# Attention block on one core: half of each head's third probability tile goes through TensorE, and two engines copy it out

## The chip, the cores and the metric

The kernel runs on one core of a Trainium2 chip. The metric is device time in microseconds, from the start of the program to its end, as the median of several runs. Beside the timed runs there is one profiled execution, whose trace all views below come from.

A core has five engines that run their own instruction streams and meet through semaphores: TensorE (PE; its weight loads are shown as PEld), VectorE (DVE), ScalarE (ACT), GpSimd (POOL) and SyncE (SP), which here only issues DMAs. TensorE writes to PSUM; the other data lies in SBUF.

## The reference

A block with adaptive layer norm: attention with 32 heads over a given key and value cache, then a mixer and an MLP. What matters here is the attention; x has 2048 rows of 640, q, k and v have 32 heads of 2048 rows of 128.

```python
def _A_ref(x, k_cache, v_cache, wq, wo):
    q = (x @ wq).reshape(B, Sq, H, Dh).transpose(0, 2, 1, 3)
    scores = jnp.einsum('bhqd,bhkd->bhqk', q, k_cache) * Dh ** (-0.5)
    p = _softmax(scores, axis=-1)
    o = jnp.einsum('bhqk,bhkd->bhqd', p, v_cache)
    return o.transpose(0, 2, 1, 3).reshape(B, Sq, H * Dh) @ wo
...
mod = (_silu(c) @ w_mod).reshape(c.shape[0], 6, 1, -1)
...
h = _layernorm(x, axis=-1) * (1 + ca) + sa
x = x + ga * _A_ref(h, A_k_cache, A_v_cache, A_wq, A_wo)
h = _layernorm(x, axis=-1) * (1 + cb) + sb
x = x + gb * _B_ref(h, B_w1, B_w2, B_w3, B_w4)
```

## The kernel before

**Steps and tiles.** The attention is one loop of steps `s` (L544). A head has 16 query tiles of 128 rows, so there are 512 tiles; step `s` makes the scores of tile `s` (128 rows by 2048 keys) and works on earlier tiles too. Tile `g` has the number `g % 16` within its head; "step 5 of a head" is the step that makes the scores of its tile 5.

**What a step issues**, engine by engine:

- TensorE: in each of two half steps two score matmuls of 512 keys (`qk`, L287, recorded as L294 and L15) into one half of the score buffer in PSUM, then eight matmuls of the product with V for tile `s - 8` (`pv`, L300, recorded as L307), then, in some half steps, one further piece. The piece is either one of five matmuls that make 512 columns of the next head's Q (`q_piece`, L242), or four 128x128 transposes (`t_piece`, L255, recorded as L261).
- VectorE: two passes (L588), one for each half of the scores. Each scales 1024 columns, writes them to `negS` in SBUF and keeps the row minimum. `negS` has three buffers.
- GpSimd: the smaller of the two minima (L598), and later the normalising of finished tiles (L448, L455) and their store to a scratch tensor (L462).
- ScalarE: every second step a copy of two finished output tiles out of PSUM (L579), copies out of the two small PSUM banks, then the exponential over 2048 columns (L601), which writes the probabilities `Pb` as bf16.
- SP: DMAs, in the order in which the loop adds them.

**Transposed probabilities.** `pv` needs the probabilities with keys on partitions (`PTs`). For 14 of a head's 16 tiles this is a DMA transpose from SBUF to SBUF (`transpose`, L228, recorded as L230): tiles 0 and 1, 4 and 5, 6 and 7, 8 and 9, 12 and 13, 14 and 15 in pairs, tiles 2 and 11 alone. Tiles 3 and 10 (`PE_TILES`) are transposed by TensorE in two halves of 1024 columns, three and four steps after their scores. Each half fills one of two small PSUM banks (`Oaug`, `QPp`), which the Q pieces use too, in turn (`bank`, L236). The bank is copied to `PTs` by `t_evac` (L265): by ScalarE (L270) in three of the four cases, ahead of that step's exponential; by VectorE (L272) for the second half of tile 3, after that step's two score passes (`by_dve`, L274). This VectorE copy stands at the end of step 7 of each head, once per head, and so serves as a mark in the trace.

**Q pieces.** `taken` (L276) lists the half steps, counted from 0 to 31 in a head, that hold transposes; groups of five Q pieces are put around them. A finished group is cast to bf16 by ScalarE (`q_evac`, L249, recorded as L252).

**SP's order in a head.** Pair (0, 1) and tile 2, then the K load of the next head (L213, at step 2), pair (4, 5), the load of the Q weights (L217), pairs (6, 7) and (8, 9), the V load (L222), tile 11, pairs (12, 13) and (14, 15).

**Order between engines.** `Prog._add` (L34) works out the waits from names: every operation lists the names it reads (`r`) and writes (`w`). An operation waits for the last writer of what it reads, and for the last writer and the readers of what it writes, if these are on another engine. The name of a half of a transposed tile is `("PT", slot, half)`, with ten slots (`RP`); that of a small bank is `("J", bank)`.

## Time and profile before

| what | value |
|---|---|
| median of three runs | 1581.96 us (1580.96 to 1587.68) |
| profiled execution, its own time | 1586.91 us |
| its span | 1585.1 us |
| granted TensorE clock | 0.998 |
| score passes L588, VectorE | 1024, mean 1220 ns |
| exponentials L601, ScalarE | 512, mean 2017 ns |
| P·V matmuls L307, TensorE | 8192, mean 220 ns |
| ScalarE's bank copies L270 | 96 of 1024 bf16 columns, mean 1.02 us |
| VectorE's bank copies L272 | 32 of 1024 bf16 columns, mean 686 ns |
| ScalarE's casts L252 | 128 of 512 columns, mean 0.58 us |
| transposing DMAs L230 | 256, median 7.0 us from issue to landing |

How to read it: the attention loop runs from about 40 to about 1268 us; the rest is the mixer and the MLP. A mean is the time from start to end of one instruction. Instructions of one engine overlap a little, so that the distance from one start to the next is shorter than the mean where the engine runs without a gap; that distance is read from the timeline. A transposing DMA shows two times: its entry on SP's queue, and the time from issue to landing.

### The profile page before, as it was taken

Reading aid. Unit: us, or ns where it says so; the run is one execution under the profiler, and the core shown is the slowest. Engines: PE = TensorE matmul, PEld = TensorE weight load, DVE = VectorE, ACT = ScalarE, POOL = GpSimd, SP = SyncE. Lnnn points to the kernel's source line nnn. Section 1 sums busy time; section 2 is a strip of 40 time slices with the busy share of each in tenths; the row PEclk is TensorE's granted clock in tenths of the full one; section 3 lists DMA queues with packets and bytes.
Section 4 is the critical chain, followed back from the end, with each engine's and each line's share of the span. In section 5 each row is a group of like instructions: output and inputs, shape, how many; then the busy total and the mean of one; then the engine's idle time right before and its main releaser. Section 6 shows DMA issues by size and latency. Waiting matters only on the chain.

```text
span 1585.1 us, 33308 instructions
## 1 busy us (share of the span) xinstructions
PE 1466.2 (92%) x13822; PEld 910.2 (57%) x13047; DVE 1395.5 (88%) x2463; ACT 1275.2 (80%) x1113; POOL 624.6 (39%) x1396
## 2 busy tenths in 40 slices
PE   4899998998999999899999999999999899999999
PEld 2466655655655556566566566656656655554545
DVE  6999999999999999999999999999999927667535
ACT  4999999999999999999999999999999900034230
POOL 0144444444444444444444444444444423323100
PEclk9999999999999999999999999999999999999999
DMA  9999999999999999999999999999999998735100
GB/s 294 239 235 237 239 234 231 252 231 223 240 233 236 233 242 239 235 246 233 235 244 236 239 245 237 236 244 240 242 238 243 236 245 184 157 55 141 39 25 34
DMA packets 1189435, 338.76 MB, mean 214 GB/s; under 512 B 1169888, under 2 KB 1183264, under 8 KB 1189280
## 3 DMA queue, kind: packets, MB, share of 16 engines
q1 hardware_dynamic: 1180800, 315.49, 100.0%
q0 software_dynamic: 6144, 16.79, 3.6%
q10 hardware_dynamic: 2336, 4.34, 0.8%
q8 instruction: 107, 1.75, 0.5%
q14 instruction: 48, 0.39, 0.1%
HBM read 43.48 MB, written 19.40 MB: 40 GB/s over the span
## 4 chain that ended last, share of the span: by engine, by line
DVE 26%; ACT 25%; PE 20%; DMA 17%; issue 9%; POOL 2%; SPq 0%; ACTq 0%; POOLq 0%; DVEq 0%
DVE negS L588 24%; ACT ring L601 20%; DMA ring<-ring 16%; PE Sps L532 7%; PE Sps L835 4%; ACT ring L270 2%; PE Oaug L786 2%; PE QPp L786 2%; PE Sps L771 1%; ACT kv L252 1%; PE PTp L307 1%; ACT Of L579 1%; DMA hTx<-o_scratch 1%; POOL small L598 1%; DVE ring L372 1%
## 5 line engine op out<-in xcount | busy, mean ns | idle before, releaser
L588 DVE TENSOR_SCALAR_CACHE_REDUCE negS<-Sps 128x1024 f32<-128x1024 f32 x1024 | 1178.5, 1220 | 35.2 <-PE Sps L15 34.2
L601 ACT ACTIVATE ring<-negS,small 128x2048 bf16<-128x2048 f32 x512 | 1029.7, 2017 | 25.1 <-POOL small L598 23.2
L307 PEld LDWEIGHTS PTp<-kv,ring 128*128 128x128 bf16 x8192 | 551.7, 98 | 370.2 <-DMA ring<-ring 95.2
L307 PE MATMUL PTp<-kv,ring 128*128 128x129 bf16 x8192 | 645.5, 220 | 49.5 <-DMA ring<-ring 48.9
L15 PE MATMUL Sps<-kv 128*128 128x512 bf16 x1024 | 387.9, 379 | 14.2 <-DVE negS L588 8.6
L598 POOL TENSOR_SCALAR small<-small 128x1 f32<-128x1 f32 x512 | 147.1, 287 | 633.3 <-DVE negS L588 633.2
L294 PE MATMUL Sps<-kv 128*128 128x512 bf16 x926 | 356.1, 385 | 24.3 <-DVE negS L588 12.8
L455 POOL TENSOR_SCALAR On<-Of,small 128x128 bf16<-128x128 f32 x512 | 191.6, 375 | 13.0
L294 PEld LDWEIGHTS Sps<-kv 128*128 128x128 bf16 x1024 | 98.2, 96 | 123.2 <-DVE negS L588 102.0
L448 POOL TENSOR_TENSOR small<-Of,small 128x4 f32<-128x4 f32 x128 | 133.4, 1042 | 9.8 <-ACT Of L579 9.7
L462 POOL DMA_DIRECT2D o_scratch<-On x128 | 103.1, 806 | 40.8 <-POOL On L455 37.2
L579 ACT COPY Of<-PTp 128x259 f32<-128x259 f32 x256 | 95.9, 374 | 14.1 <-PE PTp L307 14.1
L245 PE MATMUL Oaug<-hTx,kv 128*128 128x512 bf16 x264 | 100.1, 384 | 4.8 <-DVE hTx L404 4.8
L245 PE MATMUL QPp<-hTx,kv 128*128 128x512 bf16 x259 | 96.7, 378 | 3.2 <-ACT hTx L399 2.5
L716 ACT ACT_TABLE_LOAD x1 | 1.3, 1283 | 114.0 <-POOL hTx L734 114.0
L588 DVE DVE_READ_ACCUMULATOR negS<-Sps 128x1 f32 x1024 | 85.1, 83 | 0.0
L635 POOL TENSOR_SCALAR negS<-negS 128x1 f32<-128x1 f32 x48 | 24.5, 510 | 129.9 <-DVE negS L644 129.9
L532 PE MATMUL Sps<-wo,hTx 128*128 128x512 bf16 (+1 forms) x502 | 69.3, 297 | 2.7 <-DMA hTx<-o_scratch 2.2
L532 PE MATMUL Sps<-wo,negS 128*128 128x128 bf16 (+1 forms) x503 | 69.9, 298 | 0.5
L270 ACT COPY ring<-Oaug 128x1024 bf16<-128x1024 bf16 x64 | 65.3, 1020 | 0.0
L839 DVE TENSOR_TENSOR ring<-Sps,ring 128x640 f32<-128x640 f32 x15 | 12.4, 824 | 57.4 <-PE Sps L835 57.4
L649 DVE TENSOR_TENSOR ring<-Sps,mod_bc 128x640 f32<-128x640 f32 x16 | 13.1, 821 | 55.3 <-PE Sps L532 33.4
(88 smaller groups left out, 1018.3 us busy)
## 6 DMA issues: line engine op xcount, KB each, us to landing
kv<-in_A_v_cache_dram SPq DMA_DIRECT2D x32, 512.0 KB, 5.0
o_scratch<-On POOLq DMA_DIRECT2D x128, 128.0 KB, 3.9
kv<-in_A_wq_dram SPq DMA_DIRECT2D x32, 160.0 KB, 3.1
wo<-in_A_wo_dram SPq DMA_DIRECT2D x1, 5120.0 KB, 17.6
ring<-ring SPq DMA_TRANSPOSE x256, 7.0
ring<-in_A_x_dram SPq DMA_DIRECT2D x5, 640.0 KB, 7.1
ring<-in_w_mod_dram SPq DMA_DIRECT2D x1, 3200.0 KB, 14.1
out_dram<-wo SPq DMA_DIRECT2D x15, 160.0 KB, 1.8
```

Source lines behind the costliest of these rows:

```text
L15: return t.add_instruction(mybir.InstMatmult(name=t.bass.get_next_instruction_name(), ins=[t.lower_ap(rhs), t.lower_ap(lhsT)], outs=[t.low ...
L245: G.op("tensor", lambda t: t.matmul(JB[jb], wq[:, hb, q, :], hT[:, q, cc * 512:(cc + 1) * 512], start=(q == 0), stop=(q == KT - 1)), r=[(" ...
L294: ins = (t.matmul if c2 == 0 else partial(same_weights, t))(Sps[:, col:col + 512], QT[:, hb, j * 128:(j + 1) * 128], KTs[:, hb, col:col + ...
L307: ins = t.matmul(ob[:, 0:129], PTs[:, b, kt, :], Vaug[:, hb, kt, 0:129], start=(kt == 0), stop=(kt == NKT - 1))
L448: G.op("gpsimd", lambda g: g.tensor_tensor(out=rl[:, 4 * b:4 * b + 4], in0=Of[:].rearrange("p a z d -> p (a z) d")[:, 4 * b:4 * b + 4, 128 ...
L455: G.op("gpsimd", lambda g: g.tensor_scalar(out=On[:, b, z, :], in0=Of[:, 2 * b + z // 2, z % 2, 0:128], scalar1=rl[:, 4 * b + z:4 * b + z ...
L462: G.dma("gpsimd", lambda e: e.dma_start(o_scr[jj // 2:jj // 2 + 2, :, hh].rearrange("a p z d -> p a (z d)"), On[:, b].rearrange("p (a z) d ...
L532: ins = t.matmul(YB[b][:, c0:c0 + cw], OTj[pr % 2][:, 2 * hh + z, :], wo[:, hh, c0:c0 + cw], start=(hh == 0), stop=(hh == H - 1))
L579: G.op("scalar", lambda a, p=p: a.copy(Of[:, p % 4].rearrange("p z d -> p (z d)")[:, 0:259], PO[:, (p % 2) * 512:(p % 2) * 512 + 259]), r= ...
L588: G.op("vector", lambda v, half=half, s=s, r8=r8: v.tensor_scalar(out=negS[:, s % 3, half * 1024:(half + 1) * 1024], in0=Sps[:, half * 102 ...
L598: G.op("gpsimd", lambda g, r8=r8: g.tensor_scalar(out=nm[:, r8:r8 + 1], in0=nm0[:, r8:r8 + 1], scalar1=nm1[:, r8:r8 + 1], scalar2=None, op ...
L601: G.op("scalar", lambda a, s=s, r8=r8: a.activation(Pb[:, s % RP, :], negS[:, s % 3, :], ACT.Exp, bias=nm[:, r8:r8 + 1], scale=-1.0), r=[( ...
```

## The change

Each head's tile 2 (`PE_HALF = 2`) is split. Its first 1024 columns are still transposed by a DMA, in the same place of SP's order, of half the size (`transpose_half`). Its second 1024 columns are transposed by TensorE as two pieces of four 128x128 transposes in step 5 of the head, one in each half step, into one small bank. The bank is copied out in two parts (`h_evac`): ScalarE copies the first 512 columns ahead of its exponential of step 5, VectorE the other 512 after its two score passes of step 5. Both copies list `("PT", slot, 1)` as written. Half steps 10 and 11 are added to `taken`. The small banks now serve nine groups a head where they served eight.

```diff
+                PE_HALF = 2
...
+                def transpose_half(g):
+                    b = g % RP
+                    G.dma("sync", lambda e: e.dma_start_transpose(PTs[:, b, 0:8, :], ring[:, b, 0:1024]),
+                          ("t", b), r=[("Pb", b)], w=[("PT", b, 0)])
...
-                taken = [u for j in PE_TILES for u in range(2 * (j + 3), 2 * (j + 5))]
+                def h_evac(g, part):
+                    jb = bank(("t", g, 1))
+                    dst = PTs[:, g % RP, 8 + 4 * part:12 + 4 * part, :]
+                    src = JBb[jb][:, 512 * part:512 * part + 512].rearrange("p (k q) -> p k q", k=4)
+                    if part == 0:
+                        G.op("scalar", lambda a: a.copy(dst, src), r=[("J", jb)], w=[("PT", g % RP, 1)])
+                    else:
+                        G.op("vector", lambda v: v.tensor_copy(dst, src), r=[("J", jb)], w=[("PT", g % RP, 1)])
+                half_of = lambda g: 0 <= g < NG and g % NQT == PE_HALF
+
+                taken = [u for j in PE_TILES for u in range(2 * (j + 3), 2 * (j + 5))] + [2 * (PE_HALF + 3), 2 * (PE_HALF + 3) + 1]
...
+                        if half_of(s - 3):
+                            t_piece(s - 3, 1, half)
...
                     for fn, x, y in evacs:
                         if fn is q_evac or not by_dve(x, y):
                             fn(x, y)
+                    if half_of(s - 3):
+                        h_evac(s - 3, 0)
...
                     for fn, x, y in evacs:
                         if fn is t_evac and by_dve(x, y):
                             fn(x, y)
+                    if half_of(s - 3):
+                        h_evac(s - 3, 1)
...
-                        if not is_pe(s):
+                        if half_of(s):
+                            transpose_half(s)
+                        elif not is_pe(s):
```

## The prediction, made before the changed kernel ran

> **What bounds the kernel now.** I read the busy table first, then the groups, the waits, the queues, and the timeline of single heads. The page's first parts leave four candidates: TensorE, VectorE and ScalarE are each busy most of the span, and queue q1, which carries the transposes, is full.

> ```profile
> PE 1466.2 (92%) x13822; PEld 910.2 (57%) x13047; DVE 1395.5 (88%) x2463; ACT 1275.2 (80%) x1113; POOL 624.6 (39%) x1396
> ...
> q1 hardware_dynamic: 1180800, 315.49, 100.0%
> ```

> In the timeline one VectorE score pass (L588, half a tile) follows the last at 1.145 us, its busy 1.22 us overlapping. A head has 32 of them, and one bank copy (L272) that holds VectorE for 0.605 us: 32 x 1.145 + 0.605 = 37.24 us. That copy marks step 7 of each head. Its 32 occurrences are 37.2 to 40.0 us apart, 1186.8 us over 31 intervals, mean 38.28. So many heads run exactly at VectorE's floor and others are about 2 us longer. The 33 us above 31 floors are these waits:

> ```profile
> DVE negS L588 <- PE Sps L15: 34.2, 44, 2.3
> ...
> PE PTp L307 <- DMA ring<-ring: 48.9, 59, 2.0
> ```

> The P·V matmuls (L307) wait for a transposed tile, the next scores come late, and VectorE stands. The transposes are late because SP's queue runs behind the work:

> ```profile
> 864.41 2.02 SPq L213 DMA_TRANSPOSE kv<-in_A_k_cache_dram  x1
> 866.48 5.00 SPq L230 DMA_TRANSPOSE ring<-ring  x1
> 871.51 0.58 SPq L217 DMA_DIRECT2D kv<-in_A_wq_dram  x1
> 872.14 4.41 SPq L230 DMA_TRANSPOSE ring<-ring  x1
> ```

> The K load belongs to step 2, but the step-7 copy of that head was at 864.86: SP is five steps late, its entries end to end. The pair issued at 872.14 lands 7.6 us later, when the chain of waits has P·V start. One K load follows the last by 38.4 us on average. So the head's pace is set by the DMA queue, with VectorE 1 us below it, and ScalarE close: its exponentials follow each other at 1.905 us, the output copies L579 take 0.26, the Q casts L252 0.47, the bank copies L270 0.895: 16 x 1.905 + 8 x 0.26 + 4 x 0.47 + 3 x 0.895 = 37.1 us.

> **The change, part by part.** *DMA.* One single-tile transpose per head becomes half of one; number and order of SP's entries stay. A pair takes 4.1 to 4.5 us of the queue, half a tile a quarter of that, 1.0 to 1.1 us; at worst nothing, if time went by entries. The queue then needs 37.3 us a head (38.3 at worst).

> *TensorE.* Eight transposes more per head, in step 5. Four of them are shown in one row at 0.39 us, and the next matmul can start after about 0.23:

> ```profile
> 128.04 0.63 PE L307 MATMUL PTp<-kv,ring 128*128 128x129 bf16 x8
> 128.51 0.39 PE L261 MATMUL Oaug<-ident,ring 128*128 128x128 bf16 x4
> ```

> Scores 0.44, P·V 0.47, transposes 0.23: 1.14 us per half step, just inside VectorE's 1.145. Half steps 10 and 11 carry no other piece now, and blocking them moves no Q piece (the third group of five starts at 16 either way). I take nothing, covered by VectorE; uncovered it is 2 x 0.23 us a head, 15 us. [...]

> *ScalarE.* A copy of 512 bf16 columns: no row has it. Half of L270's 0.895 is 0.45, the cast of 512 f32 columns is 0.47: I take 0.47 (at most 0.895). ScalarE's work becomes 37.6 us.

> *VectorE.* A copy of 512 columns: between half of L272's 0.605 and all of it; I take 0.34. The floor becomes 37.57 us.

> *The added wait.* Both copies name ("PT", slot, 1) as written. The scheduler makes a later writer wait for an earlier one on another engine, so VectorE's copy, queued after its step 5, waits until ScalarE's is complete. ScalarE's stands behind exponential 4 and the output copy. This is where they are in a head without a DMA wait (VectorE first):

> ```profile
> 127.46 1.22 DVE L588 TENSOR_SCALAR_CACHE_REDUCE negS<-Sps 128x1024 f32<-128x1024 f32 x1
> 128.61 0.08 DVE L588 DVE_READ_ACCUMULATOR negS<-Sps 128x1 f32 x1
> ```
> ```profile
> 127.56 2.05 ACT L601 ACTIVATE ring<-negS,small 128x2048 bf16<-128x2048 f32 x1
> 129.46 0.41 ACT L579 COPY Of<-PTp 128x259 f32<-128x259 f32 x1
> 129.72 2.06 ACT L601 ACTIVATE ring<-negS,small 128x2048 bf16<-128x2048 f32 x1
> 131.62 1.06 ACT L270 COPY ring<-Oaug 128x1024 bf16<-128x1024 bf16 x1
> ```

> VectorE is through step 5 at 128.61. ScalarE's new copy would go where exponential 5 starts, 129.72, and be complete some 0.56 later (the casts' length); with 0.05 of signal VectorE copies at 130.33, 1.72 us late. In the heads that had a DMA wait ScalarE had caught up, and the same reckoning gives 1.0 to 1.1. Behind the waiting copy stand all of VectorE's score passes: step 6, then exponential 6, TensorE's scores of step 7.

> Does it repeat at full price? I follow one head from the moment VectorE's copy starts (0). VectorE ends step 6 at 0.34 + 2.29 = 2.63, step 7 at 4.92, step 8 (after L272) at 7.81, then every 2.29 up to step 5 of the next head at 37.57. An exponential starts at least 0.51 after its step ends (866.61 + 1.145 to 868.26 in another head). ScalarE runs exponential 5 and the copy of tile 3 until 2.66, waits 0.5 for step 6, 0.1 for 7, about 1.0 for 8, 0.1 for 9, then is never idle again: the casts, the two copies of tile 10 and the output copies put it behind. 37.6 of work and 1.75 idle bring its new copy's end to 39.3. The two engines, each with about 37.6 us of work, now meet once a head and cannot lend each other their slack: period about 39.35 us, 1.8 us of it VectorE's wait.

> *The sum*, against the profiled execution (span 1585.1, its own time 1586.9): 31 x (39.35 - 38.28) = +33.2; first head's step 5, 0.81 + 0.34 = +1.2; the DMA wait of the last eight steps goes, -1.1. The queue at 37.3 (or 38.3) is faster than 39.35, so its lag is gone by the end: the last pair is issued at 1273.0 while its exponential ended about 1268.1, -5 us in the tail (0 at least). Together +28: 1615 from this execution, 1610 from the median of the runs, 1582.0, which is 5 us lower. The new pace holds no DMA waits, the likely source of that spread, so I go between: **1612 us**. By bounds: copies at half length take 2 to 3 us off (1607), no tail gain adds 5.

> **Rivals.** *Relief wins.* If VectorE's copy waited for nothing, the new floor would be 37.57, above the relieved queue: 31 x (37.57 - 38.28) = -22, tail and rest -6: about 1556. For it: the queue is the bound now. Against: even with ScalarE starved, exponential 4 starts 0.51 after step 4, and 0.51 + 1.905 + 0.26 + 0.56 + 0.05 is 1.0 us after step 5; the two halves share one writer key. [...]

> *Short wait.* If ScalarE keeps catching up, the wait is 1.05: period 38.6, 31 x 0.35 = +11, less 5: 1588 to 1593. For it: 19 of the 32 heads show about that lag now. Against: they show it because DMA waits held VectorE back, and these go.

> *Long copies.* If small copies cost nearly as much as whole ones, 0.27 and 0.43 more per head both lie on the meeting path: +22, about 1634. A queue that is still late at times would add less. For it: nothing measured at 512 bf16 columns; against: the casts at 0.47.

> **Chances.** Forecast 0.66 (1600 to 1621), relief 0.10, short wait 0.14, long copies 0.10. A range of 1588 to 1625 holds the forecast, most of the short wait and part of the long copies: 0.8. A difference under 0.5%, 8 us, can't be told from none here. Faster by more: 0.11 (relief). Within: 0.07 (half of the short wait). Slower: 0.82.

> **What would show it.** VectorE's new copy x32 with about 1.7 us idle before each, released by ScalarE (some 50 us); ScalarE's idle before L601 up from 25 to about 70 us, released by GpSimd (L598); P·V's DMA waits and VectorE's waits for scores nearly gone; step-7 copies evenly 39.3 apart; SP waiting for ScalarE in earnest. I am wrong if that idle is under 0.3 us each, or if the DMA waits stay as they are.

## The result and the profile after

The changed kernel takes 1630.77 us (1628.73 to 1632.19, five runs) against 1583.02 us: ratio 1.029, 95% interval 1.0268 to 1.0311. It is slower, as forecast, but by 48 us where I had 30, and the time lies above the range. The profiled execution has a span of 1630.0 us, 44.9 us more than before.

The busy table and the queues:

```profile
PE 1524.3 (94%) x14327; PEld 959.7 (59%) x13303; DVE 1408.8 (86%) x2495; ACT 1292.3 (79%) x1145; POOL 622.3 (38%) x1396
...
q1 hardware_dynamic: 1148032, 307.10, 93.4%
```

The transposing queue is no longer full, yet the kernel is slower: something else bounds it. The groups (busy us, mean ns of one, idle time before them and what ended it):

```profile
L607 DVE TENSOR_SCALAR_CACHE_REDUCE negS<-Sps 128x1024 f32<-128x1024 f32 x1024 | 1178.5, 1221 | 14.7 <-PE Sps L15 14.1
L622 ACT ACTIVATE ring<-negS,small 128x2048 bf16<-128x2048 f32 x512 | 1030.6, 2021 | 56.0 <-POOL small L619 54.6
...
L322 PE MATMUL PTp<-kv,ring 128*128 128x129 bf16 x8192 | 660.0, 224 | 1.1 <-ACT Of L596 1.1
```

P·V (now L322) waits for no DMA any more, where it waited 48.9 us. VectorE waits 14 us for scores instead of 34. ScalarE stands idle for 56 us before its exponentials, nearly all of it for the minima that GpSimd makes; before, it was 25:

```profile
L601 ACT ACTIVATE ring<-negS,small 128x2048 bf16<-128x2048 f32 x512 | 1029.7, 2017 | 25.1 <-POOL small L598 23.2
```

The table of waits has a new line, VectorE's copy waiting for ScalarE's, 32 times, 1.66 us each:

```profile
DVE ring L288 <- ACT ring L286: 53.2, 32, 1.8
```

In the timeline of one head, first VectorE, then ScalarE:

```profile
528.87 0.08 DVE L607 DVE_READ_ACCUMULATOR negS<-Sps 128x1 f32 x1
530.66 0.42 DVE L288 COPY ring<-Oaug 128x512 bf16<-128x512 bf16 x1 [1.71 <-ACT ring L286]
531.00 1.21 DVE L607 TENSOR_SCALAR_CACHE_REDUCE negS<-Sps 128x1024 f32<-128x1024 f32 x1
```
```profile
527.82 2.06 ACT L622 ACTIVATE ring<-negS,small 128x2048 bf16<-128x2048 f32 x1
529.72 0.42 ACT L596 COPY Of<-PTp 128x259 f32<-128x259 f32 x1
529.98 0.65 ACT L286 COPY ring<-Oaug 128x512 bf16<-128x512 bf16 x1
530.45 2.07 ACT L622 ACTIVATE ring<-negS,small 128x2048 bf16<-128x2048 f32 x1
```

VectorE is through step 5 at 528.87. ScalarE's copy starts behind exponential 4 and the output copy, ends at 530.63, and VectorE copies at 530.66. The copies cost 0.34 us (530.66 to 531.00) and 0.47 us (529.98 to 530.45).

The step-7 copies of VectorE are 39.78 us apart on average, against 38.28 before. But they aren't even: 39.35 in the first two heads, later about 39.46, 39.86 and 40.13 in turn. In the two that take longer VectorE waits for scores again, once in step 7 (0.57 us at 256.06) or twice in step 8 (0.16 us each, at 297.64 and 299.04). TensorE's timeline shows why (the head of the two views above; the second and third line have the same shape of matmul):

```profile
529.92 0.38 PE L266 MATMUL QPp<-ident,ring 128*128 128x128 bf16 x4
532.28 0.39 PE L309 MATMUL Sps<-kv 128*128 128x512 bf16 x1 [1.98 <-DVE negS L607]
...
535.40 0.63 PE L309 MATMUL Sps<-kv 128*128 128x512 bf16 x1
```

While VectorE stands, TensorE has nothing to do for 1.98 us. Three microseconds later the same matmul takes 0.63 instead of 0.39 us. Windows of 1 us, first from a head in which this does not happen, then from the head before it, in which it does (the last three columns are the granted clock, the DMA share and the GB/s):

```profile
core 0: us, PE busy (x) PEld busy (x) DVE busy (x) ACT busy (x) POOL busy (x), PEclk, DMA share, GB/s
...
453.00:454.00 1.00, 1.00 (x15) 0.83 (x13) 1.00 (x3) 0.96 (x2) 0.01 (x1) 1.00 0.23 49
454.00:455.00 1.00, 1.00 (x15) 0.74 (x13) 1.00 (x3) 0.70 (x1) 0.61 (x2) 1.00 0.82 190
...
413.00:414.00 1.00, 1.00 (x15) 0.80 (x13) 1.00 (x3) 0.98 (x2) 0.00 (x0) 1.00 1.21 262
414.00:415.00 1.00, 1.00 (x8) 0.53 (x5) 1.00 (x3) 0.67 (x1) 0.62 (x2) 0.57 0.96 218
415.00:416.00 1.00, 1.00 (x13) 1.00 (x10) 1.00 (x3) 1.00 (x1) 0.00 (x0) 0.50 1.25 286
416.00:417.00 1.00, 1.00 (x6) 0.34 (x4) 0.91 (x3) 0.97 (x3) 0.62 (x2) 0.50 1.22 280
417.00:418.00 1.00, 1.00 (x11) 0.74 (x8) 0.92 (x1) 1.00 (x1) 0.78 (x1) 0.72 1.19 273
```

The granted clock is halved from 414.1 to 417.6. The 44.9 us of span are thus: 31 x (39.34 - 38.28) = 33 for the meeting of the two engines, 31 x 0.44 = 13 to 14 on top, which I put down to the clock, and -1.4 for the ends.

### The profile page after: what moved, and what is told of

It reads as the page before. It is cut to its first block, busy times and chain, and to the rows that moved or that the text cites. A ratio compares the mean times of both kernels' runs of the same rounds, so it can differ in the third digit from the quotient of the medians.

```text
span 1630.0 us, 34069 instructions
## 1 busy us (share of the span) xinstructions
PE 1524.3 (94%) x14327; PEld 959.7 (59%) x13303; DVE 1408.8 (86%) x2495; ACT 1292.3 (79%) x1145; POOL 622.3 (38%) x1396
## 4 chain that ended last, share of the span: by engine, by line
ACT 56%; PE 24%; DVE 14%; issue 4%; POOL 1%; DMA 0%; ACTq 0%; POOLq 0%
ACT ring L622 45%; DVE negS L607 11%; PE Sps L547 9%; ACT kv L257 4%; ACT ring L275 4%; PE Sps L858 3%; ACT Of L596 3%; PE PTp L322 2%; PE QPp L809 2%; PE Oaug L809 2%; PE Sps L794 1%; PE Sps L309 1%; PE Sps L15 1%; ACT ring L286 1%; DVE ring L288 1%
## 5 line engine op out<-in xcount | busy, mean ns | idle before, releaser
L322 PEld LDWEIGHTS PTp<-kv,ring 128*128 128x128 bf16 x8192 | 572.8, 100 | 294.9 <-issue 83.7
L322 PE MATMUL PTp<-kv,ring 128*128 128x129 bf16 x8192 | 660.0, 224 | 1.1 <-ACT Of L596 1.1
L309 PE MATMUL Sps<-kv 128*128 128x512 bf16 x1024 | 401.2, 392 | 80.4 <-DVE negS L607 77.1
L15 PE MATMUL Sps<-kv 128*128 128x512 bf16 x1024 | 395.4, 386 | 0.0
L250 PE MATMUL Oaug<-hTx,kv 128*128 128x512 bf16 x320 | 121.7, 385 | 1.9 <-ACT hTx L414 1.3
L250 PE MATMUL QPp<-hTx,kv 128*128 128x512 bf16 x320 | 120.7, 381 | 2.7 <-ACT hTx L414 2.3
L477 POOL DMA_DIRECT2D o_scratch<-On x128 | 103.1, 806 | 40.8 <-POOL On L470 37.2
L547 PE MATMUL Sps<-wo,hTx 128*128 128x128 bf16 (+1 forms) x512 | 70.7, 299 | 0.0
L266 PE MATMUL QPp<-ident,ring 128*128 128x128 bf16 x640 | 65.2, 227 | 0.0
L266 PE MATMUL Oaug<-ident,ring 128*128 128x128 bf16 x640 | 64.7, 226 | 0.0
```

Source lines behind the costliest of these rows:

```text
L15: return t.add_instruction(mybir.InstMatmult(name=t.bass.get_next_instruction_name(), ins=[t.lower_ap(rhs), t.lower_ap(lhsT)], outs=[t.low ...
L250: G.op("tensor", lambda t: t.matmul(JB[jb], wq[:, hb, q, :], hT[:, q, cc * 512:(cc + 1) * 512], start=(q == 0), stop=(q == KT - 1)), r=[(" ...
L266: ins = t.transpose(JBb[jb][:, z * 128:(z + 1) * 128], Pb[:, g % RP, kt * 128:(kt + 1) * 128], ident[:])
L309: ins = (t.matmul if c2 == 0 else partial(same_weights, t))(Sps[:, col:col + 512], QT[:, hb, j * 128:(j + 1) * 128], KTs[:, hb, col:col + ...
L322: ins = t.matmul(ob[:, 0:129], PTs[:, b, kt, :], Vaug[:, hb, kt, 0:129], start=(kt == 0), stop=(kt == NKT - 1))
L547: ins = t.matmul(YB[b][:, c0:c0 + cw], OTj[pr % 2][:, 2 * hh + z, :], wo[:, hh, c0:c0 + cw], start=(hh == 0), stop=(hh == H - 1))
```

## The experiments

Theory W: VectorE's wait for ScalarE's copy sets a head's length, and the gap that it leaves in TensorE's work halves TensorE's clock for a while. Theory T: TensorE, with eight transposes more and no slack in a half step, is the bound, and its clock is low because it has more work. Each run stands beside runs of the kernel before on the same chip; ratios are to those. The runs are from several chips, so two versions are compared by their ratios; a ratio of 0.01 is about 16 us.

**1. VectorE's copy one step later.** By then ScalarE's copy is long done.

```diff
-                    if half_of(s - 3):
-                        h_evac(s - 3, 1)
+                    if half_of(s - 4):
+                        h_evac(s - 4, 1)
```

> VectorE's copy of the 512 columns moves behind its passes of step 6, everything else as in the changed kernel. Theory W (the wait of VectorE for ScalarE's copy costs the time, and TensorE, idle for 2 us behind it, then runs at a lower granted clock): no wait before the copy, granted clock back at 0.99 or more, period of a head 37.6 us, 1555 to 1572 us, faster than before. Theory T (eight more transposes overload TensorE, whose half step had no slack, and lower its clock): period still above 39, clock near 0.97, 1620 us or more. If the copies themselves cost more than 0.34 and 0.47 us: between, 1575 to 1600.

Measured: 1575.02 us, ratio 0.9958 (0.9941 to 0.9974), clock 0.998. Of the 31 heads 13 take 37.55 us, where the forecast's floor for VectorE was 37.57; the mean is 37.91. What is left above the floor are DMA waits, as the lines of its table of waits show:

```profile
PE PTp L322 <- DMA ring<-ring: 18.8, 38, 1.1
...
DVE negS L607 <- PE Sps L15: 14.7, 21, 2.2
```

All transposes, copies and the relief of the queue are the changed kernel's; only the place of one copy differs, and the ratio falls from 1.029 to 0.996, by some 53 us. T falls. The time is 3 us above the range that W had, and at the edge of the one for dearer copies; but the heads at 37.55 us show that the copies cost what was forecast. What W had left out are the DMA waits, which did not vanish (see run 5).

**2. and 3. TensorE kept busy in its gap.** The second half of the scores of step 6 is made again, with the same values, while TensorE would stand idle: four times more in run 2, whose edit is shown, and once more in run 3.

```diff
                         if half_of(s - 3):
                             t_piece(s - 3, 1, half)
+                        if half_of(s - 4) and half == 1:
+                            for _ in range(4):
+                                qk(s, 1)
```

> The changed kernel; TensorE makes the second half of the scores of step 6 four times more (1.7 us, same values), in the gap in which it stands idle. Theory W: VectorE's wait of 1.7 us stays, TensorE's gap shrinks from 2.0 to about 0.3 us, the clock stays at 0.99 or more, all heads take 39.35 us: 1614 to 1620 us, 13 us under the changed kernel. Theory T: more work for TensorE, the same or a lower clock, 1631 us or more. If the extra 0.43 us a head comes from neither: 1629 to 1633.

Measured: 1620.36 us, ratio 1.0239 (1.022 to 1.0258), clock 0.997. More work for TensorE, and by the ratios some 8 us less than the changed kernel. W's range ended at 1620.

> The run that kept TensorE busy, with one repetition of the scores instead of four: TensorE's gap is then about 1.55 us, between 1.97 (the changed kernel, clock halves in two heads of three) and 1.30 (the wait alone, all heads alike). If the gap's length decides and 1.55 is short enough: 39.34 us in every head, 1618 to 1622 us. If any such gap lets the clock fall: 1629 to 1633.

Measured: 1616.14 us, ratio 1.023 (1.0211 to 1.025), 2 us below the range expected for a gap that is short enough. The views of the cores and of the waits:

```profile
core 0: 1613.8 us, clock 0.998
```
```profile
DVE ring L288 <- ACT ring L286: 53.1, 32, 1.8
```

VectorE's wait is the same to 0.1 us in all, but nearly every head takes 39.34 us in both runs, and the clock holds (1.00 from 60 to 1280 us in run 3, 0.97 from 60 to 1290 us in the changed kernel). So the 0.44 us a head are the clock's, and the gap of 1.97 us is what lowers it; with one pair of matmuls in it, 0.43 us, the gap is about 1.54 us (an estimate, 1.97 - 0.43), and the clock stays up. The 4 us between the two runs lie outside the 31 measured heads (39.35 and 39.34 us), almost all of them behind the last step-7 copy (339.0 against 335.3 us to the end); the cause is not known, and the ratios do not tell the two runs apart.

**4. The wait alone.** The kernel before, with all its DMA transposes, plus two copies of one column with the same place as target.

```diff
+                    if s < NG and j == 5:
+                        G.op("scalar", lambda a: a.copy(sd[:, 0:1], mone[:, 0:1]), r=["mone"],
+                             w=["X"] + [("sd", cc) for cc in range(NQC)])
...
+                    if s < NG and j == 5:
+                        G.op("vector", lambda v: v.tensor_copy(sd[:, 0:1], mone[:, 0:1]), r=["mone"], w=["X"])
```

> The kernel before, with all its DMA transposes and no further TensorE work; in step 5 of each head ScalarE copies one column ahead of its exponential and VectorE copies one column after its passes, both into the same place, so that VectorE waits for ScalarE as in the changed kernel. Theory W: VectorE idles 1.3 to 1.5 us a head for ScalarE, period 38.8 us without and 39.3 us with clock dips, DMA waits nearly gone though the DMA work is whole, 1598 to 1615 us. Theory T: no more TensorE work, so within 0.5% of before (1575 to 1591).

Measured: 1600.08 us, ratio 1.0111 (1.0094 to 1.0128), clock 0.997.

```profile
DVE small L601 <- ACT small L586: 35.2, 32, 1.3
...
PE PTp L307 <- DMA ring<-ring: 13.1, 24, 1.1
...
DVE negS L591 <- PE Sps L15: 12.2, 12, 3.3
```

Without one more TensorE transpose and without a column copied for use, the order alone costs 18 us. 26 of the 31 heads take 38.67 or 38.68 us. Where a DMA wait still makes VectorE stand for scores, its wait for ScalarE is shorter by it (0.80 us for scores, then 0.54 for ScalarE in one head; 1.30 for ScalarE in heads without), and the head's length is the same: ScalarE's chain sets it. TensorE's gap is 1.30 us at the most here, and its clock stays up (1.00 from 60 to 1260 us), which the expectation had left open.

**5. The relief alone.** The kernel before with half a DMA transpose for tile 2 from the second head on (`transpose_half` as in the changed kernel), and the second half left out, so that its place keeps older probabilities.

```diff
...
-                        if not is_pe(s):
+                        if s % NQT == 2 and s > NQT:
+                            transpose_half(s)
+                        elif not is_pe(s):
```

> The kernel before, with only the first half of tile 2 transposed by the DMA from the second head on; the second half is left out, so its slot keeps older probabilities. No copy, no TensorE transposes, no wait. If the queue's time goes by bytes (theory W's 1.0 us a head): the DMA waits shrink, period 37.3 to 37.6 us, 1553 to 1563 us. If it goes by entries: 1580 to 1587.

Measured: 1569.18 us, ratio 0.9916 (0.9899 to 0.9933): between the two.

```profile
PE PTp L311 <- DMA ring<-ring: 30.5, 49, 1.8
...
DVE negS L592 <- PE Sps L15: 19.5, 23, 3.3
```

The mean head falls from 38.28 to 37.71 us, by 0.57, and not to 37.3. The halved entry itself is as cheap as forecast: SP's entry ahead of the K load takes 1.35 us where it took 2.39 (medians of the distance to the next entry). But 21 of the 31 heads still take more than VectorE's floor of 37.22 us, because of DMA waits, and why these take back nearly half of the relief is not shown. All that the smaller transpose has to give is 12 us.

**6. and 7. One engine makes the whole copy.** `h_evac` copies 1024 columns in one instruction, on VectorE after its passes in the first of these runs, on ScalarE ahead of its exponential in the second; the other engine's call is taken out.

```diff
-                    dst = PTs[:, g % RP, 8 + 4 * part:12 + 4 * part, :]
-                    src = JBb[jb][:, 512 * part:512 * part + 512].rearrange("p (k q) -> p k q", k=4)
+                    dst = PTs[:, g % RP, 8:16, :]
+                    src = JBb[jb].rearrange("p (k q) -> p k q", k=8)
...
-                    if half_of(s - 3):
-                        h_evac(s - 3, 0)
```

> The changed kernel, but VectorE copies all 1024 columns in one instruction after its passes of step 5 and ScalarE copies none: the same transposes and DMAs, no meeting of the two engines. Theory W: no wait before the copy, no TensorE gap, clock 0.99 or more; VectorE's floor is 36.63 + 2 x 0.605 = 37.84 us a head, with some DMA waits 37.9 to 38.1: 1573 to 1582 us. If the copying as such were too much for VectorE and ScalarE: over 1600.

Measured: 1569.85 us, ratio 0.9945 (0.9931 to 0.9959), clock 0.997; heads of 37.82 us at the least, 38.08 on average in the profiled execution, which at 1578 us was the slowest of ten. The time is a little below what was expected.

> The changed kernel, but ScalarE copies all 1024 columns in one instruction ahead of exponential 5 and VectorE none. Theory W: no wait of VectorE for a copy; ScalarE has 37.1 + 0.9 = 38.03 us of work a head and is the bound, VectorE waits now and then for a buffer of negated scores: period 38.0 to 38.4, 1575 to 1588 us, clock 0.99 or more. If copying as such were the cost: over 1600.

Measured: 1575.8 us, ratio 0.997 (0.9953 to 0.9988), clock 0.997; most heads 38.04 us, where the sum of ScalarE's work was 38.03. The full copying work on one engine is cheaper than half of it on each with a meeting, by 51 to 55 us (ratios 0.997 and 0.9945 against 1.029).

**8. The engines take turns by head.** The copy of 1024 columns, made in one instruction as in runs 6 and 7, goes to VectorE in even heads, to ScalarE in odd ones.

```diff
...
-                    if half_of(s - 3):
+                    if half_of(s - 3) and h % 2:
                         h_evac(s - 3, 0)
...
-                    if half_of(s - 3):
+                    if half_of(s - 3) and not h % 2:
                         h_evac(s - 3, 1)
```

> The changed kernel, but the two engines take turns by head: in even heads VectorE copies all 1024 columns after its passes of step 5, in odd heads ScalarE copies them ahead of exponential 5. They never meet over one bank. Theory W: the two engines' floors average (37.84 + 37.24) / 2 = 37.54 and (37.13 + 38.03) / 2 = 37.58 us a head, below the DMA queue, which now sets the pace at about 37.7 to 37.9: 1566 to 1573 us, no TensorE gap. If turns bring their own waits (a head of ScalarE at 38.03 followed by one of VectorE at 37.84): 1573 to 1582.

Measured: 1574.26 us, ratio 0.9947 (0.9927 to 0.9967). Many heads take 37.22 and 38.09 us in turn, mean 37.90. The longer ones are 0.25 us above the 37.84 of VectorE's own work, so that the turns bring a small wait, as the second of the two expectations had it. By ratio it is no better than VectorE alone, and not told apart from the late copy: runs 1, 6 and 8 all beat the kernel before by about half a per cent, run 7 by 0.3%. In the profiles of runs 1 and 8 P·V still waits 18.8 and 16.3 us for DMAs; in runs 6 and 7 most heads run at the floor of the engine that copies.

## Why the prediction was right and where it was wrong

- **What bounded the kernel before: right.** Relieving the queue alone makes it faster (run 5), and in every run without the meeting VectorE, ScalarE or DMA waits give the length of a head. The reading that many heads run exactly at VectorE's floor was too strong: 5 of the 31 take 37.22 us, and the others are spread from 37.4 to 40.0.
- **The added wait: right, in place, size and repetition.** Forecast 1.72 us to start with and 1.8 repeated; the profile has 1.70 or 1.71 us of idle time in 29 of the 32 heads, and 39.35 us for the first heads, the number of the forecast. Runs 2 and 3 show it in all heads, run 4 shows that the order alone does it, run 1 that without it the cost goes. ScalarE's idle time before its exponentials rose to 56 us, less than the 70 that were named as a sign, and the copies were not evenly apart, for the reason that follows.
- **The two copies: right.** 0.34 and 0.47 us.
- **TensorE: here the prediction failed.** It said of TensorE "I take nothing, covered by VectorE", and asked only whether TensorE could keep up. It did not follow VectorE's stall to the engine behind it. VectorE's 1.7 us are 1.97 us without work for TensorE, after which its clock is halved for about 3.4 us in two heads of three. The scores then come late, and that costs 0.44 us a head on average, 13 to 14 us in all: most of the 16.6 us by which the span grew beyond the sum's +28.3. With the clock kept up by one repeated pair (run 3) it is 1616 us, beside the sum from the profiled execution, 1615, or 1619 by its ratio to the median of before; both are inside the range. The wait was known and its length too. The trace of before has one gap in P·V as long as this one:

```profile
458.21 0.64 PE L307 MATMUL PTp<-kv,ring 128*128 128x129 bf16 x8 [1.98 <-DMA ring<-ring]
```

  Behind it the clock stayed at 1.00, so that this row would have spoken for no cost (the last section has gaps of the same length that went either way). No row showed such a gap in every head; a price from both sides belonged in the range.
- **The tail: too generous.** Forecast -5 us, and -1.1 for a DMA wait of the last steps. From the last step-7 copy to the end there are 337.8 us instead of 339.6, so that the ends gave 1.4 us in all where the sum had 4.9. The queue's first load behind the last pair did come earlier, 9.2 us after VectorE's last pass ended instead of 12.6, but the rest of the tail took most of that back. From 1400 to 1500 us the clock is 0.98 where it was 1.00 before; that this is the cause is not shown. The first head's extra step cost 0.4 us, not 1.2.
- **The middle value was shaded the wrong way.** I went from 1615 towards the lower median of the runs. As the new pace holds no DMA waits, there was no reason to.
- **The rival "relief wins": refuted, and mis-sized.** The wait is there. Even without it (run 1) the gain is 0.4%, not 26 us: half a tile takes 1.04 us off its own entry in the queue, as forecast, but only 0.57 us off the mean head. "Short wait" is refuted by the first heads, "long copies" by the copies' own rows.

## What to carry to other kernels

Two engines with nearly equal work need the buffers between them; a point at which one must wait for the other each round takes that freedom away. Here it cost 1.7 us of waiting a head, where the two copies together take 0.81. The copy paid, and by half a per cent at the most, only where the second part stood where the first is long done, or where one engine made all of it. When an engine is forecast to stall, follow the stall to the engine that it feeds, and ask what an idle gap there does to that engine's speed.

## What the runs showed of the hardware

In the changed kernel the granted clock fell to 0.50 behind 19 of the loop's 30 gaps of 1.97 to 2.09 us in TensorE's work; gaps of about 1.54 us (run 3, estimated as 1.97 - 0.43) and of 1.30 us at the most (run 4) left nearly every head alike and the mean clock at 0.998 and 0.997.

```profile
core 0: us, PE busy (x) PEld busy (x) DVE busy (x) ACT busy (x) POOL busy (x), PEclk, DMA share, GB/s
410.73:414.14 3.41, 1.44 (x18) 0.96 (x14) 2.92 (x6) 3.25 (x3) 0.12 (x1) 1.00 1.09 189
414.14:417.55 3.41, 3.41 (x23) 2.35 (x21) 3.23 (x6) 3.19 (x3) 1.45 (x5) 0.50 1.14 262
448.28:451.69 3.41, 2.55 (x33) 1.83 (x28) 1.71 (x6) 3.41 (x5) 1.33 (x4) 1.00 1.26 258
451.69:455.10 3.41, 2.29 (x29) 1.75 (x27) 3.41 (x7) 3.06 (x3) 0.62 (x2) 1.00 0.84 190
```

The first gap lies whole in one stretch, and the next runs at 0.50; the second is split, 0.86 and 1.12 us, and the clock stays up. So it is in all of the loop's 30 gaps of this length: whole in one stretch 19 times, each with a fall, split 11 times, none with a fall, even where 1.95 us lay in one stretch (the gap at 93.27). The fall thus came 2.42 to 2.49 or 3.25 to 3.35 us after the gap's start, or not at all. The gap of 1.98 us in the trace of before had 1.88 us in one stretch, if its clock record is cut in the same way (the clock rises to 1.00 at 34.86 us, and 124 times 3.4133 us later is 458.11).

The turn of three fits this grid: 39.46 + 39.86 + 40.13 = 119.45 us are 35 of its stretches (35 x 3.413 = 119.46), so that after three heads the gap lies in the same place of a stretch, and in one head of three it is split between two. That the place decides is read from these positions; no run moved the gap on its own.
